# Decay terms of the first attention jobs by matmuls, and earlier loads of the later jobs, in a decay-attention and softplus-FFN kernel

## The chip, the cores and the metric

The kernel runs on one core of one Trainium2 chip. A core has TensorE (PE; matmuls and, beside them, weight loads), VectorE (DVE), ScalarE (ACT), GpSimd (POOL) and SyncE (SP, which here only issues DMA transfers). The metric is the time of one execution on the device, in microseconds; of several executions the median is taken.

## The reference

Attention with a decay over 8 batches of 8 heads, 576 tokens and a head size of 64, and then a feed-forward network with softplus over all 4608 tokens, 512 to 2048 to 512. q, k and f come in float32, the weights in float64. Cut to what is computed:

```
log_f = log(clip(f, 1e-4, 1));  cum = cumsum(log_f, -1)
scores = q @ k^T / 8 + cum[i] - cum[j],  -1e9 above the diagonal
attn = softmax(scores);  x = attn @ v          (heads side by side)
h = x @ w_in;  g = max(h, 0) + log1p(exp(-|h|));  out = g @ w_out
```

## The kernel before

**Numbers.** Most products are split into high and low parts of a faster format (fp32r) and made of two or three matmuls. At the start, while the weights are still arriving, "plain" jobs work in full float32 instead, in which a matmul takes two passes in the trace (a matmul of a transposition one).

**Weights.** w_in and w_out are float64. `load_f64` fetches a piece of 128 x 512 as pairs of words (0.5 MB a piece, 16 of each) into one of five staging buffers and makes float32 of it in five steps: `scale` on ScalarE (L444), `clip` (L447), `low` on GpSimd (L460), `sign` on ScalarE (L464), `join` on VectorE (L468). Later each piece is split into high and low parts (`copy`, L215, into `wih`, and a subtraction, L515).

**Jobs.** Attention is a row of jobs, each with its query tiles. A query tile makes scores (`s`, L787), takes their masked minimum on VectorE (L794; signs are turned, so the minimum is that of the negative scores) and their exponential on ScalarE (L814). Then the weights are turned by matmuls with the identity (`b`, L895, with the reciprocal sums by L899), copied from PSUM (L215) and multiplied by the values (`o`, L968); a product on VectorE (L991) writes x. Batch 0 is cut into three kinds of plain jobs:
- two *first* jobs: 4 heads at once, the first 128 tokens (in the code `quad`)
- four *second* jobs: 2 heads, tokens 128 to 256 (`pair`)
- eight *rests*: one head, tokens 256 to 576, query tiles of 64, 128 and 128 rows; a rest's values came in three steps, one for each bank of turned weights

The other 56 jobs are whole heads in split form. The FFN on the first two blocks of 128 tokens is plain too (up L1158, down L1281), and its up-projections need four converted pieces of w_in at a time. All later blocks are split (L1177, L1262).

**The decay.** f is loaded, clipped (L360), its logarithm taken (L363) and summed along each row by scans on VectorE (first 256 columns L376, the rest L381). `cum["x"]` holds three planes, -8, the sums and 8. Two rows of it are copied by DMA beneath q and k in the tile `T`, as rows 64 and 65, so that a score matmul over 66 rows adds the decay by itself: L691 for the first jobs (two transfers for four heads), L674 for a rest (two transfers).

**The order.** Everything is collected as operations with costs, waits and buffers, and `Plan.run` writes each engine's instructions in the order that its own estimates of their times give; the hardware then runs each engine in that order. Where the planner expects TensorE to wait more than 0.5 us, until the first down-projection, it puts in fill matmuls (`fill`, L1492), which compute nothing. Three `warm` matmuls (L1481) compute nothing either. Transfers are issued by SyncE in order, and an issue that has to wait holds up those behind it. When weight pieces are asked for is set by `W_EACH` at the end of the program.

Of the kernel before, what the change touches and what calls it, by code (L numbers as in the profile page):

```python
# [24 lines left out]
SCALE_BIAS = 1.0  # L25
# [25 lines left out]
class Plan:  # L51
# [109 lines left out]

def on_pe32(n):

    return On("PE", 4 * n / 2400 + 0.004)

# [53 lines left out]
def tile_decay_attention_softplus_ffn(  # L219
# [129 lines left out]

    decay_ready, cum_used, first_rows, cum = {}, [], [], {}  # L350

    def decay():
# [18 lines left out]

        def scan(e):

            c = cum[0]
            x = box["f"][:, 0:256]
            e.tensor_tensor_scan(c[:, 0:256], x, x, 0.0, ALU.add, ALU.min)  # L376

        def scan_rest(e):
            c = cum[0]
            x = box["f"][:, 256:S]  # L380
            e.tensor_tensor_scan(c[:, 256:S], x, x, c[:, 255:256], ALU.add, ALU.min)  # L381

# [39 lines left out]
    def load_f64(src, new, name, takes=()):  # L422
# [29 lines left out]
        def low(e):  # L452
            box["x"] = new()
            out = halves_of(box["x"], 2)[:, :, 0]
            x = halves_of(box["s"].rearrange("p c t -> p (c t)"), 4)[:, :, 1]
            scale, bias = 2.0**-13, 2.0**-14 - 0.5
            if e is nc.scalar:
                e.activation(out, x, AF.Copy, scale=scale, bias=bias)
            else:
                e.tensor_scalar(out, x, scale, bias, ALU.mult, ALU.add)  # L460

# [141 lines left out]
    def attention(job):  # L603
# [65 lines left out]
        def load32():  # L669
            def qk(e):  # L670
                e.dma_start(out=qk32[0:64], in_=qkT[b, :, heads[0]])

            def rows(e, x):
                e.dma_start(out=qk32[64 + x : 65 + x], in_=cum["x"][bh : bh + 1, 1 - x : 3 - x])  # L674

            start = add(NO_ENGINE, mark, takes=("T0",), lag=0.0)
            x = add_dma(qk, 288, after=[start] + first_rows)
            y = [
                add_dma(lambda e, r=r: rows(e, r), 4, after=[start, decay_ready["sums"]] + first_rows)
                for r in range(2)  # L680
            ]
            cum_used.append(add(NO_ENGINE, mark, after=y))
            st["T"] = [x] + y

        def load_quad():
# [81 lines left out]
        def stat_tile(ti):  # L767
# [12 lines left out]
            for i, (a, z, acc) in enumerate(pieces):  # L780
# [3 lines left out]
                def scores(e, box=box, a=a, z=z):  # L784
                    o = box["o"] = bank("att", f"s{n}_{ti}_{a}")[0:n_q, 0 : z - a]
                    if plain:
                        e.matmul(o, part32(0, q0, end), part32(1, a, z), start=True, stop=True)  # L787
                        return
                    e.matmul(o, qA[:, q0:end], kA[:, a:z], start=True, stop=False)  # L789
                    e.matmul(o, qB[0:ST, q0:end], kB[0:ST, a:z], start=False, stop=True)  # L790

                def row_min(e, box=box, w=z - a, i=i, final=final):
# [61 lines left out]
        def weights(bi):  # L854
# [68 lines left out]
            need = list(dict.fromkeys(need)) + halves_set  # L923
            m = add(on_turn(len(blocks) - 0.48 * small + 2 * len(sums)), turn, after=need, takes=("att",))
            st.setdefault("turned", []).append(m)
# [17 lines left out]
        def output_tiled():  # L943

            steps = [[] for _ in banks]
            for gi, (g0, g1, r, c0) in enumerate(groups):
# [10 lines left out]
                for m in mms:  # L957
                    m.update(start=m is mms[0], stop=m is mms[-1])
            box, before = {}, []
            for i, step in enumerate(steps):  # L960
# [3 lines left out]
                def values(e, i=i, step=step):  # L964
# [10 lines left out]
                op = add(  # L975
                    on_pe32(max(sum(m["z"] - m["a"] for m in ms) for ms in sides)), values,
                    after=list(dict.fromkeys(x for m in step for x in m["ready"])) + before + st["V"],
                    takes=("att",) if i == 0 else (),
                )
                before = [op]  # L980
                used[i].append(op)

# [111 lines left out]
    def ffn_block(i):  # L1094
# [48 lines left out]
        def up_part(u, k, half):  # L1143
# [41 lines left out]
            else:  # L1185
                need = st["load"]
            op = add(
                on_pe32(NCC * nt) if plain else on_pe(nt, 6), mm,
                after=st["split"] + need + st["ups"][-1:],
# [292 lines left out]

    give("h", [add(On("PE", 0.75 * WARM), warm, takes=("h",), after=mask_set)])

# [11 lines left out]
    for n in range(len(jobs) + 1):  # L1496
# [89 lines left out]
```

## Time and profile before

| | us |
|---|---|
| median of 3 runs | 1182.69 (1180.13 to 1183.42) |
| the profiled execution's own time | 1187.69 |
| its span, first to last instruction | 1185.9 |
| TensorE busy | 1170.5 (99%) |
| VectorE, ScalarE busy | 799.8 (67%), 832.1 (70%) |
| GpSimd busy | 127.7 (11%) |

The page gives busy time of each engine and the chain of work that ended last. Groups of lines give an operation's busy time, mean duration and the idle time before it. A timeline row has start, length, engine, line, operation, tiles, shape and count; matmuls are counted in passes. Busy time of TensorE includes fills, and a matmul's end is modelled.

### The profile page before, as it was taken

Reading aid. Unit: us, or ns where it says so; the run is one execution under the profiler, and the core shown is the slowest. Engines: PE = TensorE matmul, PEld = TensorE weight load, DVE = VectorE, ACT = ScalarE, POOL = GpSimd, SP = SyncE. Lnnn points to the kernel's source line nnn. Section 1 sums busy time; section 2 is a strip of 40 time slices with the busy share of each in tenths; the row PEclk is TensorE's granted clock in tenths of the full one; section 3 lists DMA queues with packets and bytes.
Section 4 is the critical chain, followed back from the end, with each engine's and each line's share of the span. In section 5 each row is a group of like instructions: output and inputs, shape, how many; then the busy total and the mean of one; then the engine's idle time right before and its main releaser. Section 6 shows DMA issues by size and latency. Waiting matters only on the chain.

```text
span 1185.9 us, 19896 instructions
## 1 busy us (share of the span) xinstructions
PE 1170.5 (99%) x6378; PEld 971.7 (82%) x6378; DVE 799.8 (67%) x1991; ACT 832.1 (70%) x1981; POOL 127.7 (11%) x139
## 2 busy tenths in 40 slices
PE   9999999999999999999999999999999999999998
PEld 7766779878888888888888888888888888888887
DVE  6877898877787678776776678667866773223322
ACT  5877787877886787677867777778767773444543
POOL 4211121110111011110000101001011010000000
PEclk9999999989999999999999999999999999999999
DMA  8856575555566555665566546656566433211210
GB/s 245 243 158 201 163 206 153 143 135 161 156 183 179 174 152 157 181 182 160 147 198 189 149 137 201 179 148 172 149 186 175 137 107 122 89 44 46 89 54 36
DMA packets 120776, 180.39 MB, mean 152 GB/s; under 512 B 22944, under 2 KB 80320, under 8 KB 120672
## 3 DMA queue, kind: packets, MB, share of 16 engines
q1 hardware_dynamic: 120648, 179.11, 52.5%
q8 instruction: 51, 0.84, 0.3%
q14 instruction: 53, 0.43, 0.1%
q10 hardware_dynamic: 24, 0.02, 0.0%
HBM read 109.98 MB, written 35.95 MB: 123 GB/s over the span
## 4 chain that ended last, share of the span: by engine, by line
PE 92%; DVE 4%; ACT 2%; DMA 1%; issue 1%; SPq 0%; POOL 0%; DVEq 0%; ACTq 0%; POOLq 0%
PE h L1177 31%; PE acc L1262 30%; PE b L895 8%; PE o L1027 7%; PE s L789 3%; PE s L790 3%; PE acc L1281 2%; PE h L1158 2%; PE s L787 2%; PE fill L1492 1%; PE o L968 1%; DMA T<-T 1%; ACT p L814 1%; DVE s L794 1%; DVE xl L1129 0%
## 5 line engine op out<-in xcount | busy, mean ns | idle before, releaser
L814 ACT ACTIVATE p<-s,negm 128x288 f32<-128x288 f32 (+7 forms) x384 | 183.3, 480 | 67.7 <-DVE negm L794 65.0
L1177 PE MATMUL h<-xh,wih 128*128 128x512 f32 (+1 forms) x576 | 229.9, 402 | 0.1
L1177 PE MATMUL h<-xl,wih 128*128 128x512 f32 (+1 forms) x576 | 217.7, 381 | 0.0
L794 DVE CUSTOM_DVE_ANT_0 s<-s,cmask 128x288 f32<-128x288 f32 (+6 forms) x320 | 138.0, 440 | 96.7 <-PE s L790 86.8
L1224 DVE SCALAR_TENSOR_TENSOR h<-h,e 128x512 f32<-128x512 f32 x136 | 95.8, 704 | 128.8 <-ACT e L1216 127.7
L844 POOL TENSOR_SCALAR p<-p,rsum 128x448 f32<-128x448 f32 (+4 forms) x85 | 95.1, 1127 | 763.6 <-DVE rsum L828 342.0
L1210 ACT ACTIVATE e<-h 128x512 f32<-128x512 f32 x144 | 86.0, 597 | 120.7 <-PE h L1177 116.5
L1262 PE MATMUL acc<-woh_dt_float32r,gh 128*128 128x512 f32 x376 | 153.1, 407 | 0.0
L1177 PE MATMUL h<-xh,wl 128*128 128x512 f32 (+1 forms) x576 | 149.0, 381 | 0.0
L1262 PE MATMUL acc<-woh_dt_float32r,gl 128*128 128x512 f32 x376 | 147.3, 392 | 0.1
L1262 PE MATMUL acc<-wol_dt_float32r,gh 128*128 128x512 f32 x376 | 146.9, 391 | 0.0
L921 DVE TENSOR_TENSOR pl<-b,ph 128x512 fp32r<-128x512 f32 x168 | 111.0, 666 | 21.0 <-ACT ph L215 17.8
L1177 PEld LDWEIGHTS h<-xh,wl 128*128 128x128 f32 x576 | 105.3, 189 | 21.5
L1177 PEld LDWEIGHTS h<-xh,wih 128*128 128x128 f32 x576 | 109.7, 190 | 15.7 <-PE b L895 0.3
L1177 PEld LDWEIGHTS h<-xl,wih 128*128 128x128 f32 x576 | 109.8, 191 | 14.8 <-DVE xl L1129 0.2
L1232 DVE TENSOR_TENSOR gl<-h,gh 128x512 fp32r<-128x512 f32 x136 | 93.6, 688 | 41.3 <-ACT gh L215 38.9
L895 PE MATMUL b<-ident,p 128*128 128x128 f32 (+1 forms) x728 | 118.5, 270 | 2.7 <-ACT p L215 1.7
L215 ACT CAST ph<-b 128x512 fp32r<-128x512 f32 (+2 forms) x167 | 82.1, 493 | 45.2 <-PE b L895 39.6
L215 ACT CAST gh<-h 128x512 fp32r<-128x512 f32 x113 | 66.4, 588 | 60.5 <-DVE h L1224 41.3
L895 PEld LDWEIGHTS b<-ident,p 128*128 128x128 f32 (+1 forms) x728 | 87.0, 139 | 19.3 <-issue 3.6
L789 PE MATMUL s<-T 128*64 128x64 f32 x336 | 97.6, 304 | 4.7 <-DMA T<-T 2.0
L790 PE MATMUL s<-T 68*64 68x64 f32 x336 | 98.0, 296 | 0.1
(153 smaller groups left out, 2224.0 us busy)
## 6 DMA issues: line engine op xcount, KB each, us to landing
wl<-wil_d SPq DMA_DIRECT2D x72, 512.0 KB
T<-T SPq DMA_DIRECT2D x224, 144.0 KB
raw<-in_qkT SPq DMA_DIRECT2D x112, 144.0 KB
g_d<-gh SPq DMA_DIRECT2D x84, 128.0 KB
g_d<-gl SPq DMA_DIRECT2D x84, 128.0 KB
vr<-in_vR SPq DMA_DIRECT2D x64, 160.0 KB
out<-ob SPq DMA_DIRECT2D x36, 256.0 KB
sto<-in_w_out SPq DMA_DIRECT2D x11, 512.0 KB
```

What stands on the lines that cost most here:

```text
L215: (e.tensor_copy if hasattr(e, "tensor_copy") else e.copy)(out, in_)
L789: e.matmul(o, qA[:, q0:end], kA[:, a:z], start=True, stop=False)
L790: e.matmul(o, qB[0:ST, q0:end], kB[0:ST, a:z], start=False, stop=True)
L794: e.tensor_tensor_reduce(out=box["o"], in0=box["o"], in1=cmask[0:n_q, right - w : right], scale=-0.125, scalar=m0 if i else 3.0e38, op0=AL ...
L814: e.activation(o, box["o"], AF.Exp, bias=m1, scale=-1.0, accum_out=acc)
L844: e.tensor_scalar(a, a, f_, None, ALU.mult)
L895: e.transpose(box["ps"][0 : x.shape[1], at : at + one.shape[1]], x, one)
L921: e.tensor_sub(box["l"], box["ps"][:, 0:w], box["h"].bitcast(F32))
L1177: e.matmul(o, l, r, start=m == 0, stop=m == 11)
L1224: e.scalar_tensor_tensor(h, h, 0.0, box["e"], ALU.max, ALU.add)
L1232: e.tensor_sub(box["l"], box["t"], box["h"].bitcast(F32))
L1262: e.matmul(st["acc", tt], l, r[fc], start=first and m == 0, stop=last and m == 2,)
```

## The change

Five things are changed.

First jobs: the score matmul runs over 64 rows, q and k alone, and two further matmuls into the same bank add the decay: the sums' tile `cum` as the stationary operand against a row of an 8-times identity that is spread over 128 columns, and a spread row of a -8-times identity as the stationary operand against `cum`. Both are float32, 64 rows deep and 128 columns wide; four tiles in two jobs make sixteen of them. They wait for a scan of the first 128 columns alone; the scan is now in three pieces (128, 128, 320). The two rows in `T` are still written for these heads, since the second jobs read them.

Rests: their two rows come in one transfer. Their first query tile multiplies 128 columns of queries instead of 64; the minimum and what follows use the first 64 rows, as before. Their values are one step, after all banks, instead of three.

Loads: before the first rest, one weight piece is asked for per job instead of two.

Planner: no fill before TensorE's first instruction; other costs for `warm`, for `low` (which now also reserves the port that it shares with VectorE), for values, for turned sums and for plain up-projections. `clip` may only go to VectorE, and `low` only to GpSimd.

```
-                elif op.start - clock["PE"] > 0.5:
+                elif clock["PE"] and op.start - clock["PE"] > 0.5:
...
+    eye8 = [cpool.tile([BH, BH], F32, name=f"eye8{x}") for x in "pm"]
+    eye8_set = [
+        add(
+            [on_act(BH), on_dve(BH, True)],
...
+        for x, v in zip(eye8, (8.0, -8.0))
+    ]
...
-        decay_ready["first"] = add(On("DVE", 0.63), scan, after=[l])
-        c = decay_ready["sums"] = add(On("DVE", 0.78), scan_rest, after=[decay_ready["first"]])
+        for x, a, z in (("quad", 0, P), ("first", P, 2 * P), ("sums", 2 * P, S)):
+            on = On("DVE", 0.11 + (z - a) / 480)
+            c = decay_ready[x] = add(on, lambda e, a=a, z=z: scan(e, a, z), after=[c])
...
-        on = [On("POOL", 1.95), on_dve(512, True, bias=SCALE_BIAS)]
-        cl = add(on, clip, after=[sc])
-        lw = add(On("POOL", 1.95), low, after=[ld], takes=takes)
+        cl = add(on_dve(512, True), clip, after=[sc])
+        lw = add(On("POOL", 0.85, 0.0, True), low, after=[ld], takes=takes)
...
             if quad:
-                return heads32(heads[a // P], 1)[0:ST0, 0, which, 0:P]
+                return heads32(heads[a // P], 1)[0:64, 0, which, 0:P]
...
-            def rows(e, x):
-                e.dma_start(out=qk32[64 + x : 65 + x], in_=cum["x"][bh : bh + 1, 1 - x : 3 - x])
+            def rows(e):
+                x = cum["x"][bh : bh + 1, 0:2]
+                planes = bass.AP(x.tensor, x.offset, [x.ap[0], [S, 2], [S, 2], [1, S]])
+                e.dma_start(out=qk32[64:ST0], in_=planes)
...
-            st["T"] = T_of[heads[0]] = T_of[heads[2]] = x + y
+            st["T"] = x
+            T_of[heads[0]] = T_of[heads[2]] = x + y
...
-                        e.matmul(o, part32(0, q0, end), part32(1, a, z), start=True, stop=True)
+                        e.matmul(
+                            o, part32(0, q0, q0 + P), part32(1, a, z), start=True, stop=not quad,
+                        )
...
+                def sums(e, box=box, h=heads[ti % len(heads)]):
+                    c, (plus, minus) = cum[0][:, 0:P], (x[:, h : h + 1].to_broadcast([BH, P]) for x in eye8)
+                    e.matmul(box["o"], c, plus, start=False, stop=False)
+                    e.matmul(box["o"], minus, c, start=False, stop=True)
...
+                if quad:
+                    o = add(on_pe32(2 * P), sums, after=[o, decay_ready["quad"]] + eye8_set)
+                    cum_used.append(o)
...
+            if not quad and not pair:
+                steps = [sum(steps, [])]
...
-            for _ in range(W_EACH if n >= nfirst else W_EACH - 1):
+            for _ in range(W_EACH if n >= nfirst else 1):
```

**Where the order moves.** Names in the rows are tiles with a running number: `s` scores, `T` the q/k tile, `b` turned weights, `o` outputs, `x` attention's result, `sti`, `sto`, `xh_st`, `xl_st` staging buffers, `ti`, `to` pieces on their way, `woh`, `wol` the float32 pieces of w_in and w_out.

TensorE, the start of the program; before:

```order
L1492 MATMUL fill<-cmask 128x128 x4
L1481 MATMUL warm<-cmask 128x448 x3
L1492 MATMUL fill<-cmask 128x128 x13
L787 MATMUL s_0_0_183<-T_72 128x128
L787 MATMUL s_1_128_185<-T_72 128x128
L787 MATMUL s_2_256_187<-T_72 128x128
L787 MATMUL s_3_384_192<-T_72 128x128
L1492 MATMUL fill<-cmask 128x128 x2
L787 MATMUL s_0_0_201<-T_72 128x256
```

The same place in the changed kernel:

```order
L1495 MATMUL warm<-cmask 128x448 x3
L787 MATMUL s_0_0_154<-T_72 128x128
L805 MATMUL s_0_0_154<-eye8p,cum 128x128
L806 MATMUL s_0_0_154<-cum,eye8m 128x128
L787 MATMUL s_1_128_161<-T_72 128x128
L805 MATMUL s_1_128_161<-eye8p,cum 128x128
L806 MATMUL s_1_128_161<-cum,eye8m 128x128
```

The seventeen early fills are gone, and each score of a first job has its two products behind it. In the whole program 3 fill matmuls are left of 58.

SyncE, from the weight pieces six and seven on (the first rest's load is L671, its rows L674, its values L652); before:

```order
L440 DMA sto_321<-in_w_out 128x1024
L440 DMA sto_351<-in_w_out 128x1024
L440 DMA xh_st<-in_w_out 128x1024
L440 DMA xh_st<-in_w_in 128x1024
L440 DMA xl_st<-in_w_in 128x1024
L440 DMA sti_457<-in_w_in 128x1024
L671 DMA T_72<-in_qkT 64x1152
L674 DMA T_72<-cum 1x16x72 x2
L652 DMA vr_499<-in_vR 128x320
```

The same place in the changed kernel:

```order
L444 DMA sto_316<-in_w_out 128x1024
L444 DMA sto_342<-in_w_out 128x1024
L670 DMA T_72<-in_qkT 64x1152
L675 DMA T_72<-cum 2x1x1152
L651 DMA vr_392<-in_vR 128x320
L444 DMA xh_st<-in_w_out 128x1024
L670 DMA T_72<-in_qkT 64x1152
L675 DMA T_72<-cum 2x1x1152
L651 DMA vr_444<-in_vR 128x320
L444 DMA xh_st<-in_w_in 128x1024
L670 DMA T_73<-in_qkT 64x1152
L675 DMA T_73<-cum 2x1x1152
```

The first rest's load now stands behind the seventh weight piece, before behind the eleventh, with one transfer of rows; the last three pieces of the second group of w_in come after the third rest's load.

VectorE, ahead of the first rest's first minimum (the last row of each piece); before:

```order
L468 SCALAR_TENSOR_TENSOR wol_dt_float_435<-to_447,wol_dt_float_435 128x512
L794 ISA s_1_256_466,negm_76<-s_1_256_466,cmask 128x256
L794 ISA negm_76 128x1
L991 TENSOR_TENSOR x_0_261<-o_473,p_1_471 128x128
L447 TENSOR_SCALAR ti_481<-ti_481 128x512
L468 SCALAR_TENSOR_TENSOR woh_dt_float_459<-ti_461,woh_dt_float_459 128x512
L827 SCALAR_TENSOR_TENSOR lsum_80<-lsum_80,part_84 128x2
L828 RECIPROCAL rsum_88<-lsum_80 128x2
L215 CAST wih<-woh_dt_float_459 128x512
L447 TENSOR_SCALAR ti_495<-ti_495 128x512
L468 SCALAR_TENSOR_TENSOR woh_dt_float_483<-ti_481,woh_dt_float_483 128x512
L794 ISA s_0_0_521,negm_77<-s_0_0_521,cmask 64x320
```

In the changed kernel:

```order
L468 SCALAR_TENSOR_TENSOR wol_dt_float_379<-to_386,wol_dt_float_379 128x512
L387 CAST ch<-cum 64x576
L388 TENSOR_TENSOR cl<-cum,ch 64x576
L468 SCALAR_TENSOR_TENSOR wol_dt_float_410<-to_402,wol_dt_float_410 128x512
L1005 TENSOR_TENSOR x_0_256<-o_374,p_1_377 128x128
L797 ISA s_1_256_439,negm_76<-s_1_256_439,cmask 128x256
L797 ISA negm_76 128x1
L797 ISA s_0_0_448,negm_77<-s_0_0_448,cmask 64x320
```

Between the first minimum of all and this row, VectorE had 11 clips, 10 joins, 4 copies into `wih` (L215) and 2 subtractions (L515), and has 7 clips, 7 joins and none of the last two; copies of turned weights are 5 instead of 4. On ScalarE up to the same tile's exponential the scalings are 8 instead of 11, the steps with the sign 7 instead of 11, the copies of turned weights 5 instead of 7, and the copies into `wih` 4 instead of 2.

More of the change, by code (lines that the diff above doesn't have):

```diff
@@ L159, in on_pe, with on_pe32 @@
     return On("PE", times * (max(n * 0.000444, m * 0.00092) + 0.002))
-def on_pe32(n):
-    return On("PE", 4 * n / 2400 + 0.004)
+def on_pe32(n, switch=False):
+    return On("PE", 4 * n / 2400 + 0.004 + 0.19 * switch)
 def on_turn(n):
@@ L350, in tile_decay_attention_softplus_ffn @@
     decay_ready, cum_used, first_rows, cum = {}, [], [], {}
+    eye8 = [cpool.tile([BH, BH], F32, name=f"eye8{x}") for x in "pm"]
+    eye8_set = [
+        add(
+            [on_act(BH), on_dve(BH, True)],
+            lambda e, x=x, v=v: e.mul(x, ident[0:BH, 0:BH], v) if e is nc.scalar
+            else e.tensor_scalar(x, ident[0:BH, 0:BH], v, None, ALU.mult),
+        )
+        for x, v in zip(eye8, (8.0, -8.0))
+    ]
     def decay():
@@ L370, in eights, with scan @@
             e.memset(cum["x"][:, t, :], value)
[L372 to L381, printed above, removed]
+        def scan(e, a, z):
+            c, x = cum[0], box["f"][:, a:z]
+            e.tensor_tensor_scan(c[:, a:z], x, x, c[:, a - 1 : a] if a else 0.0, ALU.add, ALU.min)
         def split(e):
@@ L398, in decay @@
         l = add(on_act(S), log, after=[o])
-        decay_ready["first"] = add(On("DVE", 0.63), scan, after=[l])
         decay_ready["eights"] = set_
-        c = decay_ready["sums"] = add(On("DVE", 0.78), scan_rest, after=[decay_ready["first"]])
+        c = l
+        for x, a, z in (("quad", 0, P), ("first", P, 2 * P), ("sums", 2 * P, S)):
+            on = On("DVE", 0.11 + (z - a) / 480)
+            c = decay_ready[x] = add(on, lambda e, a=a, z=z: scan(e, a, z), after=[c])
         give("wl", [c])
@@ L455, in low @@
             x = halves_of(box["s"].rearrange("p c t -> p (c t)"), 4)[:, :, 1]
[L456 to L460, printed above, removed]
+            e.tensor_scalar(out, x, 2.0**-13, 2.0**-14 - 0.5, ALU.mult, ALU.add)
         def sign(e):
@@ L671, in qk @@
                 e.dma_start(out=qk32[0:64], in_=qkT[b, :, heads[0]])
-            def rows(e, x):
-                e.dma_start(out=qk32[64 + x : 65 + x], in_=cum["x"][bh : bh + 1, 1 - x : 3 - x])
+            def rows(e):
+                x = cum["x"][bh : bh + 1, 0:2]
+                planes = bass.AP(x.tensor, x.offset, [x.ap[0], [S, 2], [S, 2], [1, S]])
+                e.dma_start(out=qk32[64:ST0], in_=planes)
             start = add(NO_ENGINE, mark, takes=("T0",), lag=0.0)
             x = add_dma(qk, 288, after=[start] + first_rows)
[L678 to L683, printed above, removed]
+            y = add_dma(rows, 9, after=[start, decay_ready["sums"]] + first_rows)
+            cum_used.append(add(NO_ENGINE, mark, after=[y]))
+            st["T"] = [x, y]
         def load_quad():
@@ L784, in scores @@
                 def scores(e, box=box, a=a, z=z):
-                    o = box["o"] = bank("att", f"s{n}_{ti}_{a}")[0:n_q, 0 : z - a]
+                    o = bank("att", f"s{n}_{ti}_{a}")[:, 0 : z - a]
+                    box["o"] = o[0:n_q]
                     if plain:
-                        e.matmul(o, part32(0, q0, end), part32(1, a, z), start=True, stop=True)
+                        e.matmul(
+                            o, part32(0, q0, q0 + P), part32(1, a, z), start=True, stop=not quad,
+                        )
                         return
+                    o = box["o"]
                     e.matmul(o, qA[:, q0:end], kA[:, a:z], start=True, stop=False)
@@ L923, in weights @@
             need = list(dict.fromkeys(need)) + halves_set
-            m = add(on_turn(len(blocks) - 0.48 * small + 2 * len(sums)), turn, after=need, takes=("att",))
+            m = add(on_turn(len(blocks) - 0.48 * small + 2 * len(sums) + 1.7 * bool(sums)), turn, after=need, takes=("att",))
             st.setdefault("turned", []).append(m)
@@ L975, in output_tiled @@
                 op = add(
-                    on_pe32(max(sum(m["z"] - m["a"] for m in ms) for ms in sides)), values,
+                    on_pe32(max(sum(m["z"] - m["a"] for m in ms) for ms in sides), True), values,
                     after=list(dict.fromkeys(x for m in step for x in m["ready"])) + before + st["V"],
@@ L980, in output_tiled @@
                 before = [op]
-                used[i].append(op)
+                for bi in range(len(banks)) if len(steps) == 1 else (i,):
+                    used[bi].append(op)
             puts = []
@@ L1187, in up_part @@
             op = add(
-                on_pe32(NCC * nt) if plain else on_pe(nt, 6), mm,
+                on_pe32(1.05 * NCC * nt) if plain else on_pe(nt, 6), mm,
                 after=st["split"] + need + st["ups"][-1:],
@@ L1481, in warm @@
             e.matmul(o[:, 0:MW], cmask[:, 0:P], cmask, start=True, stop=True)
-    give("h", [add(On("PE", 0.75 * WARM), warm, takes=("h",), after=mask_set)])
+    give("h", [add(On("PE", 1.3 * WARM), warm, takes=("h",), after=mask_set)])
     filling = []
```

## The prediction

> **What bounds the kernel now.** I read the page first: span, busy shares, the chain that ended last.
>
> ```profile
> span 1185.9 us, 19896 instructions
> PE 1170.5 (99%) x6378; PEld 971.7 (82%) x6378; DVE 799.8 (67%) x1991; ACT 832.1 (70%) x1981; POOL 127.7 (11%) x139
> PE 92%; DVE 4%; ACT 2%; DMA 1%; issue 1%; SPq 0%; POOL 0%; DVEq 0%; ACTq 0%; POOLq 0%
> ```
>
> TensorE is the bound: 99% busy, 92% of the chain. The matmuls that compute something are the same before and after, apart from sixteen new ones and the width of eight. So the time can only change where TensorE is idle, runs matmuls that compute nothing, or runs slowly. I looked for these with the windows (in each row: length, then busy time of PE, weight loads, DVE, ACT and POOL, granted clock, DMA share, GB/s) and with the groups of lines.
>
> ```profile
> 0.00:80.00 80.00, 75.79 (x535) 55.73 (x536) 62.03 (x188) 58.48 (x141) 23.40 (x41) 1.00 0.72 212
> 80.00:140.00 60.00, 60.00 (x409) 41.74 (x409) 48.09 (x119) 45.45 (x101) 11.99 (x15) 1.00 0.66 192
> L1492 PE MATMUL fill<-cmask 128*128 128x128 f32 x116 | 16.5, 292 | 1.4 <-POOL cmask L314 1.4
> L1481 PE MATMUL warm<-cmask 128*128 128x448 f32 x6 | 4.2, 863 | 0.0
> ```
>
> In the first 80 us TensorE is idle for 4.2 us, fills for 16.5 and warms for 4.2: 24.9 us without result. From 80 to 140 it is never idle. What the change can win by an earlier start lies in these 24.9 us. The timeline shows where the first of them are.
>
> ```profile
> 1.39 2.07 PE L1492 MATMUL fill<-cmask 128*128 128x128 f32 x8 [1.39 <-POOL cmask L314]
> 3.26 4.19 PE L1481 MATMUL warm<-cmask 128*128 128x448 f32 x6
> 7.28 3.06 PE L1492 MATMUL fill<-cmask 128*128 128x128 f32 x26
> 10.18 1.06 PE L787 MATMUL s<-T 66*128 66x128 f32 x8
> 36.29 3.39 PE L1492 MATMUL fill<-cmask 128*128 128x128 f32 x28
> 39.62 0.75 PE L787 MATMUL s<-T 66*64 66x320 f32 x2
> 116.03 0.75 PE L787 MATMUL s<-T 66*64 66x320 f32 x2
> ```
>
> The first score starts at 10.18, the first rest's first score at 39.62, both right behind a run of fills. I take the stretches between these marks; the second ends at 116.03, where the eighth rest starts.
>
> ```profile
> 10.18:39.62 29.44, 28.07 (x225) 21.99 (x223) 26.26 (x83) 24.02 (x62) 11.07 (x12) 1.00 0.87 276
> 39.62:116.03 76.41, 74.96 (x513) 51.40 (x512) 58.37 (x149) 60.63 (x132) 17.36 (x22) 1.00 0.66 193
> ```
>
> In the first stretch VectorE is busy 89% and ScalarE 82%: with the weights' conversions between the first jobs' steps, these two set its length. In the second TensorE does.
>
> **The start.** The first scores no longer wait for the two rows that are written after the scan, only for q and k. The next rows show when these can be there (the last three are of the transfers: two sizes, and the issue of weight pieces six and seven).
>
> ```profile
> 2.00:5.50 3.50, 3.50 (x10) 2.27 (x10) 1.40 (x3) 0.69 (x2) 1.61 (x8) 1.00 0.85 206
> 1.73 0.30 POOL L335 TENSOR_SCALAR_AFFINE_SELECT cmask<-cmask 128x128 f32<-128x128 f32 x1
> 4.66 0.68 DVE L376 TENSOR_TENSOR_SCAN cum<-fs 64x256 f32<-64x256 f32 x1 [0.75 <-ACT fs L363]
> 10.73 0.30 DVE L794 CUSTOM_DVE_ANT_0 s<-s,cmask 128x128 f32<-128x128 f32 x1 [4.17 <-PE s L787]
> fs<-in_f SPq DMA_DIRECT2D x1, 144.0 KB
> T<-in_qkT SPq DMA_DIRECT2D x4, 256.0 KB
> 15.92 2.07 SPq L440 DMA_DIRECT2D sto<-in_w_out  x2
> ```
>
> By 5.5 us 3.5 x 206 = 0.72 MB have moved; f (0.15 MB) and the first two q/k transfers (0.26 each), issued first, are 0.67. The scan of 256 columns ended at 5.34, that of 128 ends sooner, so the products' new wait is over before the scores, behind which they stand. With the early fills gone, the warm matmuls start when cmask is ready, at 2.1, and take their 4.2 us to 6.3. So the first score starts at about **6.6 instead of 10.18**. The sixteen products have two passes each; 26 passes of this size took 3.06 us, 0.118 each, so 32 x 0.118 = 3.8 us of TensorE. They lie in the stretch that VectorE and ScalarE set, where fills took their place before. A tile takes 0.7 us now; the first minimum is at 7.4 instead of 10.73, VectorE having waited 4.17 us there. The eye tiles and the split scan run on engines that wait there; if that cover were gone, they would cost about 0.5 us.
>
> **The stretch to the first rest.** The rows of the order on VectorE say which conversions move behind it: from the first minimum to the first rest's, 7 clips instead of 11, 7 joins instead of 10, no copies of w_in's high part instead of 4, no subtractions instead of 2, one copy of turned weights more. On ScalarE 3 scalings, 4 steps with the sign and 2 copies of turned weights fewer, 2 copies of high parts more. Rows for their durations (least, median, largest, in ns):
>
> ```profile
> L447 DVE TENSOR_SCALAR ti<-ti x16: 409/422/993, 16.3 to 99.3; 128x512 f32<-128x512 f32 x16
> L468 DVE SCALAR_TENSOR_TENSOR woh_dt_float<-ti,woh_dt_float x16: 670/686/1176, 18.9 to 101.6; 128x512 uint32<-128x512 uint32 x16
> L215 DVE CAST wih<-woh_dt_float x9: 410/427/1035, 23.2 to 102.3; 128x512 fp32r<-128x512 f32 x9
> L515 DVE TENSOR_TENSOR wil<-woh_dt_float,wih x10: 662/683/693, 25.9 to 137.4; 128x512 fp32r<-128x512 f32 x10
> L215 DVE COPY p<-b x13: 409/553/684, 15.1 to 130.9; 128x384 f32<-128x384 f32 x9, 128x512 f32<-128x512 f32 x3, 128x256 f32<-128x256 f32 x1
> L444 ACT ACTIVATE ti<-sti x9: 667/675/682, 15.2 to 98.4; 128x512 f32<-128x512 f32 x9
> L464 ACT ACTIVATE woh_dt_float<-ti x16: 759/777/790, 17.5 to 100.7; 128x512 f16<-128x512 f32 x16
> L215 ACT COPY p<-b x23: 342/561/588, 14.3 to 132.1; 128x512 f32<-128x512 f32 x13, 128x384 f32<-128x384 f32 x7, 128x256 f32<-128x256 f32 x3
> L215 ACT CAST wih<-woh_dt_float x7: 592/619/621, 28.4 to 97.2; 128x512 fp32r<-128x512 f32 x7
> ```
>
> VectorE: 4 x 0.42 + 3 x 0.69 + 4 x 0.43 + 2 x 0.68 - 0.55 = 6.3 us less, 26.26 - 6.3 = 20.0; at the same 89%, 22.4 us. ScalarE: 3 x 0.675 + 4 x 0.777 + 2 x 0.56 - 2 x 0.62 = 5.0 less, 19.0; at 82%, 23.2 us. The larger: the first rest starts at 6.6 + 23.2 = 29.8, **9.8 us earlier**. Ends of this term: 10.6 if VectorE alone sets it; 3.6 if only the start moves and the rest keeps its 29.4 us. I take ScalarE's, the nearer to what these engines reached before. The rest's data isn't late: its load is issued behind the seventh weight piece instead of the eleventh, and pieces six and seven were issued by 18 us.
>
> **From there to the eighth rest** TensorE has the same work. Before, it lost 76.41 - 74.96 = 1.45 us idle and the fills of this row:
>
> ```profile
> 40.00:60.00 20.00, 1.87 (x12) 1.49 (x12) 1.00 0.77 230
> ```
>
> Together 3.3 us, of which I take half as gained: **1.6** (ends 0 and 3.3). Against it stand the deferred conversions: ScalarE has 60.63 + 5.0 = 65.6 us to do in about 74, 89%, a share like those at which the first stretch was held up. I charge **1.6** (ends 0 and 3). That rows go in one transfer saves an issue on SyncE per rest, whose data isn't late: nothing. A rest's values in one step wait for its last copied bank; TensorE has next scores and up-projections ahead of them in the order, and without these one copy, 0.55 us, would show per rest: nothing.
>
> The first tile of a rest now uses 128 columns of queries instead of 64. Two tiles show what the narrow one costs:
>
> ```profile
> 105.67 0.75 PE L787 MATMUL s<-T 66*64 66x320 f32 x2
> 106.36 1.98 PE L1281 MATMUL acc<-wol_dt_float,g 128*128 128x512 f32 x4
> 109.16 0.92 PE L787 MATMUL s<-T 66*128 66x448 f32 x2
> 109.92 1.02 PE L1281 MATMUL acc<-wol_dt_float,g 128*128 128x512 f32 x2
> ```
>
> Start to start, the wide tile has 0.76 us for two passes of 448, so 320 would take 0.54; the narrow one has 0.69. By eight rests the extra 0.15 and about 0.1 behind it are **2.0 us** gained (ends 0 and 2.9).
>
> **The clock.** The fills also kept TensorE busy. Where it wasn't, this happened:
>
> ```profile
> 175.00:180.00 5.00, 3.35 (x19) 3.10 (x18) 3.12 (x10) 3.32 (x10) 2.64 (x2) 0.75 0.70 202
> PE s L789 <- DMA T<-T: 2.0, 2, 1.6
> 160.00:260.00 100.00, 94.59 (x579) 83.20 (x577) 84.80 (x229) 78.55 (x207) 15.63 (x14) 0.95 0.56 152
> ```
>
> One wait of 1.6 us, and the granted clock was 0.75 over these five: TensorE stood 1.65 us and then had half its speed for a while. Between 7 and 30 us the work is 29.44, less 1.4 idle and the 9.5 us of fills there (16.5 - 2.1 - 3.1 - 1.9 elsewhere), 18.5, and 3.8 of products: 22.3 of 23.2, but in pieces. I charge **1.6 us** for a spell at half clock that isn't hidden (ends 0 and 10). The Trainium skill (TensorE: Matmul & The Clock Gate, section HAM oscillation) asks only that no gap of TensorE exceeds about 3.4 us; by it the fills can go for nothing, and the sum would be 1.6 us better. The trace differs: a wait of 1.6 was enough.
>
> **Sum:** 9.8 + 1.6 + 2.0 - 1.6 - 1.6 = 10.2 us. The profiled execution took 1187.7 us, so the changed one should take 1177.5. The median of the runs shown, 1182.69, is 5.0 lower; taken from it, the forecast is **1172.5 us**, 0.9% faster.
>
> **Rivals.**
> *The weights become the bound.* Rests load ahead of weights, and SyncE waits in order: behind a rest's load that waits for its buffer stand the pieces for the second group of up-projections. For it: the DMA share is 0.87 already in the first stretch, and that group's last pieces stand behind the third rest's load. Against it: their results are needed only after the second rest. If most of the start's gain is waited away, some 3.6 us + 2.0 stay, less the two charges: 2.4, so 1180.3.
>
> *The change doesn't do what it says:* the products take what the rows' wait gave (3.8 against 3.6) and VectorE and ScalarE hold the rest where it was. Then only the first tiles' 2.0 is left: 1180.7, within 0.3% (3.5 us), which is about what a measurement of this kernel tells from no change.
>
> *Slower: half clock through the first jobs.* Fills gone, the scattered work falls under what keeps the clock up, and stays there. Then its 22.3 us take 44.6, the first rest starts at 51.2 instead of 39.6, and less 2.0 + 1.6 the total is 8.0 us worse: 1190.7. It decides once the first rest starts later than 43.2, that is with 14.3 of the 22.3 us of work at half speed. For it: the 175 to 180 row. Against it: in that row PE was busy 67%, and from 0 to 80, without the fills, still (75.79 - 16.5) / 80 = 74%; and a slow TensorE is busier, which brings the clock back.
>
> *Another planned order later.* From 160 to 260 TensorE is idle 5.4 us and 5% of the clock is missing, 10.4 us in all. All later rows are planned anew from other times; this loss may be 5 us larger or smaller.
>
> **How the numbers follow.** Forecast, within the spread of the last rival (1167.5 to 1177.5): 0.56. More gained (10.6 at the rest, 3.3, 2.9, no charges: 16.8, so 1166): 0.10. Weights: 0.16. Only the tiles: 0.10. Half clock, or the later loss at its worst with little gained: 0.08. To hold 8 in 10, the range runs from **1165** to **1182**. Faster by over 0.3% (below 1179.1): the forecast, the better case and about half of the weights (that case loses less than all of it as often as not), 0.74; within: 0.18; slower: 0.08.
>
> **What would show it.** First score at 6 to 7 us, the first minimum 3 us earlier, the first rest's score between 28 and 33, fill time near zero, the eighth rest between 103 and 110, granted clock 1.00 in the first 40 us. The clock below that from 10 to 30 would show the slower rival; long waits of the up-projections (L1158 before) for a weight piece would show the first. If the eighth rest is 9 us earlier and the end isn't, the loss after 160 us has grown.

## The result and the profile after

| | before | after |
|---|---|---|
| median of 4 runs each | 1182.39 (1180.13 to 1183.42) | 1168.51 (1167.36 to 1168.53) |
| the profiled execution's own time | 1187.69 | 1167.36 |
| its mean granted clock | 0.995 | 0.999 |

The ratio is 0.9878, 95% interval 0.9859 to 0.9896: 13.9 us faster by the medians, where 10.2 were forecast. The page of the changed kernel, with span, busy times and the chain that ended last:

```profile
span 1165.6 us, 19711 instructions
PE 1154.2 (99%) x6300; PEld 960.4 (82%) x6300; DVE 796.9 (68%) x1992; ACT 832.6 (71%) x1984; POOL 126.8 (11%) x138
PE 85%; DVE 4%; ACT 1%; issue 0%; DVEq 0%; ACTq 0%
```

TensorE's busy time fell by 16.3 us: 110 fill passes are gone and the products' 32 are new, which is the whole difference from x6378 to x6300. Now the same stretches as before the change; the windows of the changed kernel (length, then busy time of PE, weight loads, DVE, ACT, POOL, then granted clock, DMA share, GB/s):

```profile
0.00:80.00 80.00, 76.72 (x531) 54.90 (x531) 64.05 (x194) 64.84 (x153) 23.24 (x41) 1.00 0.79 236
80.00:140.00 60.00, 58.60 (x409) 42.90 (x408) 54.38 (x142) 50.63 (x121) 12.68 (x17) 1.00 0.72 202
6.41:31.06 24.65, 23.78 (x184) 17.78 (x184) 19.25 (x72) 19.97 (x56) 7.04 (x8) 1.00 0.82 242
31.06:103.54 72.48, 72.15 (x510) 51.55 (x508) 61.18 (x159) 62.87 (x140) 20.26 (x25) 1.00 0.79 236
160.00:260.00 100.00, 98.36 (x604) 86.71 (x603) 88.62 (x238) 83.39 (x215) 14.93 (x13) 0.98 0.57 158
```

And its timeline on TensorE at the marks of the prediction (start, length, engine, line, operation):

```profile
2.08 4.40 PE L1495 MATMUL warm<-cmask 128*128 128x448 f32 x6 [2.08 <-POOL cmask L335]
6.41 0.48 PE L787 MATMUL s<-T 64*128 64x128 f32 x2
6.73 0.38 PE L805 MATMUL s<-eye8p,cum 64*128 64x128 f32 x2
6.96 0.38 PE L806 MATMUL s<-cum,eye8m 64*128 64x128 f32 x2
9.28 0.94 PE L1506 MATMUL fill<-cmask 128*128 128x128 f32 x6
30.52 1.24 PE L787 MATMUL s<-T 66*128 66x256 f32 x4
103.54 0.70 PE L787 MATMUL s<-T 66*128 66x320 f32 x2
```

The first score starts at 6.41 instead of 10.18. The first rest's first score is the second half of the row at 30.52 and starts at 31.06 instead of 39.62; the eighth rest starts at 103.54 instead of 116.03. So the gain builds up in three pieces: 3.8 us by the first score, 4.8 more to the first rest (24.65 for 29.44), 3.9 more to the eighth (72.48 for 76.41): 12.5. Of the profiled executions' other 7.8 us (spans 1185.9 and 1165.6), most lies between 160 and 260, where TensorE is idle for 1.6 us instead of 5.4 and has 0.98 of its clock instead of 0.95. But the profiled execution of before was 5.3 us above its median, so of these 7.8 only some 1.4 belong to the medians' 13.9 (13.9 - 12.5).

### The profile page after: what moved, and what is told of

The parts are those of the page before. It is cut to its first block, busy times and chain, and to the rows that moved or that the text cites. A ratio compares the mean times of both kernels' runs of the same rounds, so it can differ in the third digit from the quotient of the medians.

```text
span 1165.6 us, 19711 instructions
## 1 busy us (share of the span) xinstructions
PE 1154.2 (99%) x6300; PEld 960.4 (82%) x6300; DVE 796.9 (68%) x1992; ACT 832.6 (71%) x1984; POOL 126.8 (11%) x138
## 4 chain that ended last, share of the span: by engine, by line
PE 85%; DVE 4%; ACT 1%; issue 0%; DVEq 0%; ACTq 0%
PE h L1191 32%; PE acc L1276 31%; PE b L906 7%; PE o L1041 7%; PE s L793 3%; PE s L792 3%; PE acc L1295 1%; DVE s L797 1%; DVE xl L1143 1%; DVE pl L932 0%; DVE h L1238 0%; DVE x L1067 0%; DVE wil L514 0%; PE h L1172 0%; ACT p L825 0%
## 5 line engine op out<-in xcount | busy, mean ns | idle before, releaser
L215 ACT CAST ph<-b 128x512 fp32r<-128x512 f32 (+2 forms) x169 | 82.8, 491 | 44.3 <-PE b L906 34.6
L215 ACT CAST gh<-h 128x512 fp32r<-128x512 f32 x111 | 65.2, 587 | 58.4 <-DVE h L1238 39.1
```

The costliest lines, as they stand in the source:

```text
L215: (e.tensor_copy if hasattr(e, "tensor_copy") else e.copy)(out, in_)
```

## The experiments

Twelve kernels ran, in 4 to 12 executions each. Three questions: does the clock hang on what keeps TensorE busy at the start (theory C of the expectations); how much of the gain do the early start and the loads carry; and do the planner's side (costs, one step for a rest's values) and the first tile's width matter? Times are medians; the last columns are of the profiled execution. In e9 and e10 the first score is the first matmul that computes one, behind the matmuls without a result (dummies) that run ahead of it, and the first rest is read from the same place of the order. The ratio isn't the quotient of the medians: long executions move it (c1's medians, 1167.49 and 1182.01 for before beside it, would give 0.988).

| run | us | ratio to before, 95% | first score | first rest |
|---|---|---|---|---|
| c1, the change again | 1167.49 | 0.9905 (0.9875 to 0.9936) | 5.99 | 30.94 |
| e1, narrow first tile | 1168.29 | 0.9884 (0.9871 to 0.9896) | 6.85 | 31.92 |
| g1, more fills | 1168.81 | 0.9881 (0.9863 to 0.9898) | 6.74 | 32.85 |
| e2, without the products | 1176.06 | 0.9941 (0.9923 to 0.9960) | 6.52 | 37.52 |
| e9, dummies for the products | 1170.63 | 0.9907 (0.9887 to 0.9927) | 7.71 | 34.1 |
| e5, rows again | 1178.13 | 0.9947 (0.9924 to 0.9969) | 11.60 | 42.67 |
| e10, rows and dummies | 1173.19 | 0.9922 (0.9906 to 0.9938) | 11.47 | 35.72 |
| e4, two weight pieces per job | 1177.50 | 0.9969 (0.9947 to 0.9991) | 6.62 | 36.02 |
| e7, values in three steps | 1176.50 | 0.9946 (0.9927 to 0.9965) | 6.67 | 31.25 |
| e8, old planner costs | 1176.38 | 0.9947 (0.9933 to 0.9961) | 8.06 | 36.73 |
| e3, before without fills | 1189.16 | 1.0065 (1.0052 to 1.0078) | 9.37 | 41.61 |
| e6, before with the loads alone | 1178.65 | 0.9957 (0.9939 to 0.9974) | 10.21 | 34.38 |

### c1 and e1: the change again, and its first tile narrow

> The changed kernel as it is, beside the next three on the same chip. Both theories: about 1168.5 us, 13.9 less than before.

1166.1 to 1168.5 in six executions; three others took 1173.6, 1176.1 and 1183.1, the first two at a mean clock of 0.994 and 0.991, so the new kernel too loses its clock at times. The third had 0.999; what made it long is not known.

```
-                            o, part32(0, q0, q0 + P), part32(1, a, z), start=True, stop=not quad,
+                            box["o"], part32(0, q0, end), part32(1, a, z), start=True, stop=not quad,
```

> The changed kernel, with the first query tile of a rest 64 columns wide again; the order of all instructions stays. If the narrow tile costs 0.25 us each time (0.15 itself, 0.1 behind it), the time is 2.0 us above the changed kernel's. The rival, that those 0.25 us came from other neighbours in the trace and not from the width: within 0.5 us of the changed kernel.

1168.29 for 1168.51: no difference. From the first to the eighth rest it takes 73.3 us instead of 72.5, so the wide tile saves 0.8 us there and not the 2.0 of the prediction, and even that doesn't reach the end.

### e2 and e9: the products, as cover for the clock

e2 leaves out the sixteen products (the first jobs lack their decay) at the same order:

```
-                            o, part32(0, q0, q0 + P), part32(1, a, z), start=True, stop=not quad,
+                            o, part32(0, q0, q0 + P), part32(1, a, z), start=True, stop=True,
...
-                    e.matmul(box["o"], c, plus, start=False, stop=False)
-                    e.matmul(box["o"], minus, c, start=False, stop=True)
```

> The changed kernel without its sixteen products, so that the first jobs lack their decay; the order of all else stays. If the products lie where VectorE and ScalarE set the pace, as the prediction said, the time changes by less than 1 us. If they lie on the path, up to their 3.6 us (16 x 0.223 in the changed kernel's timeline) go.

Less work, and 8 us slower, which neither side expected. The windows of e2 show why, and below them its longest waits on TensorE between 6.7 and 33.4 us (total, times, longest):

```profile
9.60:13.01 3.41, 2.53 (x19) 1.49 (x17) 1.72 (x9) 1.64 (x7) 0.00 (x0) 0.99 0.97 241
13.01:33.49 20.48, 20.11 (x85) 12.48 (x85) 16.15 (x48) 15.05 (x36) 6.56 (x8) 0.50 0.64 213
33.49:40.00 6.51, 6.51 (x50) 4.75 (x49) 3.81 (x12) 3.88 (x10) 0.00 (x0) 1.00 0.44 131
```

```profile
PE s L787 <- DMA T<-in_qkT: 0.9, 1, 0.9
PE s L787 <- ACT p L823: 0.7, 1, 0.7
PE b L904 <- ACT p L823: 0.4, 1, 0.4
```

From 9.60 to 13.01 TensorE was busy 74%, with no wait over 0.9 us; then it ran at half clock for 20.48 us, although it was busy 98% of them. Of its six executions, one had a mean clock of 0.999 and took 1169.6, the other five 0.989 to 0.993 and 1175.5 to 1178.0: with the clock up, by this one execution, the products' absence costs 1 us at most, and the other 7 are the clock.

e9 puts two matmuls without a result ahead of each first job's score in e2:

```
+                        for _ in range(2 * quad):
+                            e.matmul(o, cmask[:, 0:P], cmask[:, 0:P], start=True, stop=True)
                         e.matmul(
                             o, part32(0, q0, q0 + P), part32(1, a, z), start=True, stop=True,
```

> The changed kernel without its sixteen products (so the first jobs lack their decay terms), with two dummy matmuls of the mask's 128 columns ahead of each of the first eight scores: TensorE gets the same amount of work at these places, none of it with a result. Theory C (the products' worth beside the start is that they keep TensorE busy enough for full clock): the clock stays 1.00 in the first 40 us, the first rest starts at 30 to 32 us, 1166.5 to 1169.5 us. Theory P (the loss of 8 us without the products came from something else than a less busy TensorE, such as another course of VectorE's minima): the clock falls to half again and it takes 1174 to 1178.

The same stretch in e9:

```profile
0.00:20.00 20.00, 17.93 (x86) 12.09 (x86) 8.57 (x43) 8.51 (x26) 6.12 (x22) 1.00 0.86 226
20.00:40.00 20.00, 19.46 (x138) 12.41 (x138) 19.17 (x62) 19.05 (x48) 4.21 (x5) 1.00 0.70 198
```

Its first score stands behind four passes of stand-ins:

```profile
6.72 1.06 PE L788 MATMUL s<-cmask 128*128 128x128 f32 x4
7.71 0.71 PE L789 MATMUL s<-T 64*128 64x128 f32 x2
```

The clock is 1.00 again and 5.4 us of the 8 come back. Of the six executions four held the clock (0.999 to 1.000, 1169.5 to 1170.7); the other two had 0.994 and 0.995 and took 1175.8 and 1173.7. The first rest comes at 34.1, later than the 30 to 32 expected: VectorE gets through 8.57 us of work in the first 20, for 11.6 in the changed kernel, so the stand-ins ahead of the scores aren't as well placed as the products behind them. So a busy TensorE is what the products give to the clock, whatever they compute; that is theory C, with a price of its own for the stand-ins and 1.1 us above the time that it expected.

### e3 and g1: the fills

e3 is the kernel before with its 58 fills left out, nothing else.

```
...
-        for _ in range(round(us / 0.215)):
-            e.matmul(filling[0][:, 0:P], cmask[:, 0:P], cmask[:, 0:P], start=True, stop=True)
+        pass
```

> The kernel before without its 58 fills, all else in the same order. Theory A, the fills overran their gaps and pushed real work back: 3 to 6 us faster than before. Theory B, the work behind them waited for data or for VectorE and ScalarE anyway: within 1 us of before. Theory C, they kept the clock up: the granted clock falls to 0.5 in windows between 10 and 40 us and the time is up to 5 us longer.

Windows of e3, and the longest wait on TensorE from 6 to 40 us:

```profile
0.00:20.00 20.00, 15.09 (x49) 9.37 (x50) 8.84 (x46) 8.88 (x28) 6.98 (x23) 0.74 0.82 242
20.00:40.00 20.00, 18.38 (x96) 13.10 (x95) 15.06 (x40) 12.84 (x30) 5.05 (x7) 0.58 0.66 185
40.00:60.00 20.00, 17.87 (x100) 12.07 (x98) 15.19 (x43) 14.52 (x33) 6.04 (x7) 0.83 0.82 246
```

```profile
PE s L787 <- DMA T<-cum: 2.8, 1, 2.8
```

Half clock for 27.3 us from 9.6 and for 6.8 from 47.2, and 7 us slower, 2 more than theory C allowed. The wait that the early fills of before covered shows bare: the first scores stood 2.8 us for the rows of the sums. So in the kernel before the fills held the clock in the first 40 us. That the clock makes up all of the 7 us isn't shown: four of the five executions had a mean clock of 0.984 to 0.986 and took 1187.7 to 1190.7, but the fifth had 0.996 and took 1190.9, the longest.

g1 has fills in the changed kernel again, wherever the planner expects 0.05 us of wait (12 instead of 3).

```
-                elif clock["PE"] and op.start - clock["PE"] > 0.5:
+                elif clock["PE"] and op.start - clock["PE"] > 0.05:
...
-        for _ in range(round(us / 0.215)):
+        for _ in range(max(1, round(us / 0.215))):
```

> The changed kernel with nine single fills more, between 16 and 45 us; the order of all else stays. If the changed kernel's few longer executions (1173 to 1183 among 1166 to 1168.5) come from the clock falling in the first 40 us, they get rarer here; the usual executions stay at 1166 to 1169, since the fills stand where TensorE waits. If the fills are on the path, all executions are up to 2 us longer (9 x 0.22).

1168.81: no gain. Its four executions lie between 1168.1 and 1170.8 at clocks of 0.999 and 1.000; four are too few to say that it never loses the clock.

### e5 and e10: the start without the products

e5 takes the decay of the first jobs from rows of `T` again, so the first scores wait for them.

```
-                return heads32(heads[a // P], 1)[0:64, 0, which, 0:P]
+                return heads32(heads[a // P], 1)[0:ST0, 0, which, 0:P]
...
-            st["T"] = x
-            T_of[heads[0]] = T_of[heads[2]] = x + y
+            st["T"] = T_of[heads[0]] = T_of[heads[2]] = x + y
...
-                if quad:
-                    o = add(on_pe32(2 * P), sums, after=[o, decay_ready["quad"]] + eye8_set)
-                    cum_used.append(o)
```

> The changed kernel, but the first jobs read their decay from the two rows beneath q and k again, without the products; loads, planner costs and all else of the change stay, and the planner puts in 15 fills. By the prediction's start term the first score falls back to about 10 us and the first rest by up to 3.6 us: 1169 to 1172. The rival, that the products' gain is only that they keep TensorE busy: fills do the same here, and the time is within 1 us of 1168.5.

10 us slower, which neither side expected, and again two kinds of executions: two of ten at a mean clock of 1.000 took 1169.4 and 1170.1, the other eight at 0.988 to 0.991 took 1175.8 to 1181.0. In the profiled one the clock is half for 23.9 us:

```profile
14.30:38.20 23.90, 23.90 (x101) 14.72 (x101) 16.30 (x53) 16.21 (x43) 6.07 (x7) 0.50 0.52 165
```

e10 adds the dummies of e9 to e5:

> The changed kernel with the first jobs' decay terms as rows of the q/k tile again, and the same two dummy matmuls ahead of each of the first eight scores. Theory C: the start is as late as with the rows alone (11 to 12 us), the clock now holds, the first rest starts at 33 to 36, and it takes 1169 to 1172: the earlier start itself is worth 1 to 4 us, and the other 8 of the 10 that the rows cost were the clock. Theory S (the earlier start is itself worth 8 us or more, and the clock is a side matter): 1175 to 1180 even with the clock at 1.00.

The timeline of e10 (fills, dummies, first score):

```profile
6.71 3.31 PE L1504 MATMUL fill<-cmask 128*128 128x128 f32 x22
9.86 0.61 PE L787 MATMUL s<-cmask 128*128 128x128 f32 x4
11.47 0.46 PE L788 MATMUL s<-T 66*128 66x128 f32 x2 [1.00 <-DMA T<-cum]
```

The clock held, and it took 1173.2, 1.2 above the range expected and 2.6 us more than e9, for a first score 3.8 us later (11.47 for 7.71). e5's two executions at full clock say 1 to 2 us. So **the earlier start itself is worth 1 to 3 us**, with the order that the planner makes of it; the other 7 to 9 that the rows cost in e5 are the clock. Theory S falls. In the profiled executions the later start is made up by the eighth rest, which starts at 107.51 in e10 and 107.72 in e9, so that the difference arises behind it; how much the start alone is worth stays open within these bounds.

### e4 and e6: the loads

e4 asks for two weight pieces per job ahead of the first rest again; e6 is before with one.

```
-            for _ in range(W_EACH if n >= nfirst else 1):
+            for _ in range(W_EACH if n >= nfirst else W_EACH - 1):
```

> The changed kernel, but two weight pieces asked for per job ahead of the first rest, as before; the planner orders anew and puts in 22 fills instead of 3. If the deferred conversions are what brought the first rest forward (the first stretch is set by VectorE and ScalarE), the first rest starts 3 to 5 us later than 31.1 and the time is about 1171 to 1174. If the start alone did it, the first rest stays within 1 us and the time at 1168.5.

> The kernel before with one part of the change alone: one weight piece per job ahead of the first rest instead of two; 36 fills instead of 58. If the deferred conversions are worth what the first stretch's sum says without the start (9.8 less 3.6), the first rest starts about 6 us earlier and the time is 1175 to 1178. If they are given back later, as they have to be done at some time, within 1.5 us of before.

e4 gives back 9 us by the medians, more than the 2.5 to 5.5 expected, and e6 wins 4 to 5. Not all of e4's 9 are the loads: five of its twelve executions, at a clock of 0.998 to 1.000, took 1174.7 to 1175.9, which is 6 to 7 us above the change; six took 1177.4 to 1183.9 at 0.991 to 0.997, and one 1189.3 at 0.999. From first score to first rest, e4 takes 29.4 us (36.02 - 6.62), e6 24.2 (34.38 - 10.21), where before took 29.4 and after 24.65: the loads alone make this stretch, independent of the products. How they do it shows on TensorE in e4:

```profile
26.36 3.84 PE L1172 MATMUL h<-x,woh_dt_float 128*128 128x128 f32 x32
33.46 2.72 PE L1506 MATMUL fill<-cmask 128*128 128x128 f32 x22
36.02 0.70 PE L787 MATMUL s<-T 66*128 66x320 f32 x2
```

and on the queue of transfers, where the first rest's q and k are issued, in e4:

```profile
27.34 0.55 SPq L670 DMA_DIRECT2D T<-in_qkT x1
```

and in the changed kernel, beside its up-projection:

```profile
17.68 0.55 SPq L670 DMA_DIRECT2D T<-in_qkT x1
```

```profile
25.43 3.84 PE L1172 MATMUL h<-x,woh_dt_float 128*128 128x128 f32 x32
```

The up-projection in front of the rest starts only 0.9 us later in e4 (26.36 for 25.43). Then the changed kernel goes on with the first rest's scores, while e4 has 26 fill passes ahead of them: q and k are issued 9.7 us later, behind four more weight pieces, and the planner expects TensorE to wait here. The trace has this transfer as 64 packets of 4608 bytes. The last of them ends at 23.55 us in the changed kernel, at 33.50 in e4 and at 33.95 in the kernel before. So in e4 the last 22 fill passes began just as q and k were there, and the scores came 2.5 us later, behind them; in the kernel before, the 28 passes began at 36.29, 2.3 us after it. Most of this term is then a wait that the planner writes into TensorE's order, and only about 1 us work that ScalarE and VectorE no longer do first. What these scores would have waited for without the fills, if for anything, no run shows.

### e7 and e8: one step for the values, and the planner's costs

```
-            if not quad and not pair:
-                steps = [sum(steps, [])]
```

> The changed kernel with a rest's values in three steps again, one per bank, in place of one; the rest planned anew from there. My theory (one step neither gains nor costs, as predicted): 1166 to 1170. Rival (switching less often between values and other work saves 0.2 to 0.4 us for each of the rests): 1171 to 1176.

8 us slower, the rival's side and just above its range. Up to the first rest nothing changes (31.25); the loss is spread behind it. Windows of e7:

```profile
20.00:60.00 40.00, 38.18 (x280) 27.29 (x280) 35.37 (x95) 34.64 (x81) 12.40 (x15) 1.00 0.75 236
60.00:140.00 80.00, 76.51 (x535) 56.34 (x536) 71.59 (x181) 63.42 (x148) 17.79 (x19) 1.00 0.71 207
140.00:260.00 120.00, 115.10 (x696) 97.24 (x695) 102.89 (x279) 97.51 (x256) 18.83 (x17) 0.99 0.58 156
```

and of the changed kernel:

```profile
20.00:60.00 40.00, 39.35 (x289) 28.21 (x288) 36.09 (x101) 35.67 (x84) 13.19 (x14) 1.00 0.73 230
60.00:140.00 80.00, 78.60 (x547) 57.57 (x546) 70.71 (x182) 68.19 (x157) 16.59 (x22) 1.00 0.74 210
140.00:260.00 120.00, 118.36 (x730) 103.19 (x729) 105.35 (x285) 100.83 (x261) 17.90 (x15) 0.99 0.60 164
```

TensorE is idle for 10.2 us in e7 and 3.7 in the changed kernel, 6.5 more of the 9.7 by which the two profiled executions differ. The waits are for many things, at most 2.1 us for any one (exponentials, values' copies, a high part). Little of the loss lies in the rests themselves. The first job behind them starts in e7 at

```profile
116.81 0.59 PE L792 MATMUL s<-T 128*64 128x64 f32 x1
```

and in the changed kernel, 2.7 us earlier, at

```profile
114.08 0.59 PE L792 MATMUL s<-T 128*64 128x64 f32 x1
```

The other 6.9 of the 9.6 us between the spans (1175.2 and 1165.6) come behind this place. The rival's reason, less switching in each rest, would put the loss in the rests; this speaks for the other order of TensorE that the planner writes for all that follows. A run with one step and the old order was not made, so the two were not separated.

e8 has the planner's old numbers:

```
-    return On("PE", 4 * n / 2400 + 0.004 + 0.19 * switch)
+    return On("PE", 4 * n / 2400 + 0.004)
...
-        lw = add(On("POOL", 0.85, 0.0, True), low, after=[ld], takes=takes)
+        lw = add(On("POOL", 1.95), low, after=[ld], takes=takes)
...
-    give("h", [add(On("PE", 1.3 * WARM), warm, takes=("h",), after=mask_set)])
+    give("h", [add(On("PE", 0.75 * WARM), warm, takes=("h",), after=mask_set)])
```

and likewise the old fill rule, turn and up-projection.

> The changed kernel with the planner's old costs and rules (fill rule, switch, low half of a weight, turn of the sums, up-projections); the work is the same, the order is planned from the old numbers, with 30 fills of 128 columns instead of 3. Theory L (the gain comes from the products and the loads; the costs matter by 3 us at most): 1167 to 1171. Rival (the new costs set a better order, by which much of the gain after 160 us comes): 1173 to 1180.

The rival's time again, 8 us, but not at its place: it looked behind 160 us, and most of the loss is at the start. Windows and timeline of e8:

```profile
8.06:36.73 28.67, 27.01 (x215) 21.98 (x215) 22.16 (x70) 19.87 (x54) 8.41 (x8) 1.00 0.71 198
```

```profile
1.40 2.08 PE L1506 MATMUL fill<-cmask 128*128 128x128 f32 x8 [1.40 <-POOL cmask L314]
3.26 3.98 PE L1495 MATMUL warm<-cmask 128*128 128x448 f32 x6
7.08 1.05 PE L1506 MATMUL fill<-cmask 128*128 128x128 f32 x8
8.06 0.48 PE L787 MATMUL s<-T 64*128 64x128 f32 x2
```

Fills ahead of the warm matmuls and behind them make the first score 1.65 us later, though its data doesn't call for it, and the stretch to the first rest is 4.0 longer. Which of the costs does the latter was not tried.

**Taken together** the parts don't add up: undone one at a time, the loads, the one step and the costs each give back 8 to 9 us (the loads 6 to 7 where the clock holds), and the products 8 to 10, mostly through the clock, of a gain of 13.9. Each part needs the others to be worth what it is; no version that ran is measurably faster than the change.

## Why the prediction was right, and where it wasn't

**The start** held: 6.41 for 6.6, and the scan and the first minimum stand where they were put. VectorE in the changed kernel:

```profile
4.67 0.42 DVE L383 TENSOR_TENSOR_SCAN cum<-fs 64x128 f32<-64x128 f32 x1 [0.75 <-ACT fs L372]
7.50 0.30 DVE L797 CUSTOM_DVE_ANT_0 s<-s,cmask 128x128 f32<-128x128 f32 x1 [0.69 <-PE s L806]
```

The sums were there at 5.1, before the scores, and the minimum came at 7.50 for 7.4. That the sixteen products are hidden held too (e2 at full clock). What the term left out: of 3.8 us gained at the start, 1 to 3 reach the end (e10, e5).

**The stretch to the first rest** was forecast at 23.2 us and took 24.65: 8.6 us gained at the first rest for 9.8. ScalarE had 19.97 us of work at 81%, close to the 19.0 at 82% of the sum. But the reason was only partly right. The sum divides ScalarE's work by its busy share, as if its conversions alone held the first rest; e4, with the old loads, shows 0.9 us of later work and 3.4 us of fills. The step "the rest's data isn't late" was true of the changed kernel and, by the packets, of the kernel before when its 28 fill passes began: these passes were the planner's. The number came out because the same edit removes both, which is luck as far as this reason goes.

**From there to the eighth rest** 3.9 us were gained for a net 2.0. The terms: fills and idle time gave 3.0 (fills gone, idle 0.33 for 1.45), not half of 3.3; the deferred conversions cost nothing visible (ScalarE busy 87%, TensorE idle 0.33 us), not 1.6; the narrow tile was 0.8 by e1's stretch, not 2.0, about 0.1 for each of eight rests where 0.25 was charged, and nothing of it reaches the end.

**The clock** was the right worry. The changed kernel ran at 1.00 through the first 140 us, so the 1.6 us charged weren't paid there; c1's two executions at 0.991 and 0.994 show that a spell can still come. What averts it in most executions is the products themselves: without them (e2, e5) the clock was half for 20 to 24 us in most executions, and 7 us or more were lost. The slower rival's mechanism exists, but smaller than priced: it had all of the first jobs' work at half speed and the first rest at 51.2, and it needed one later than 43.2 to be slower than before. The spells of e2 and e5 covered most of that stretch, and the first rest came at 37.5 and 42.7. Its counter-argument, that a slow TensorE is busier and so the clock comes back, failed: e2 was busy 98% of a spell of 20.48 us.

**"A rest's values in one step: nothing"** is the step that failed: e7 puts it at 8 us. The argument looked at one rest alone, at what its values wait for, and not at what the planner does with TensorE's order afterwards. **The planner's new costs** weren't priced at all; e8 puts them at 8 as well. Both sit in the rival "another planned order later", which was given 5 us either way and no side.

**The weights** never became the bound: TensorE's waits for a plain up-projection (L1172) are 0.3 us in all from 20 to 260, put down to VectorE and not to a weight piece. So the forecast of 1172.5 missed by 4.0 us, on the side of too little, from the two charges that weren't paid, the fills' other half and the later stretches; its parts were less independent than a sum of terms makes them look. That it came this close is partly luck: two parts that give back 8 us each when undone stood in the sum at nothing or not at all.

## What to carry to other kernels

Matmuls without a result that fill TensorE's waits are not waste until the same place is shown to stay busy without them: remove the wait and the fills together, or put real work there, and look at the granted clock. When loads are put into another order, look in the old order at when the data landed and whether fills still stand ahead of its reader then: fills follow the planner's estimate, and not the transfer. Where a planner writes the order, changed costs and merged steps are edits of their own, with effects as large as those of the work they describe, and worth a run each before the parts are added up.

## What the runs showed of the hardware

The granted clock fell to half for multiples of 3.41 us: 20.48 in e2 (six times 3.41), 27.3 and 6.8 in e3 (eight and two), 23.9 in e5 (seven). In the 3.41 us before e2's spell TensorE was busy 74%, with one wait of 0.9 us; in e4 3.41 us that were busy 58% (64.41 to 67.82, with a wait of 1.4) had full clock behind them. So neither a least busy share nor a longest wait can be read from these rows. At half clock, e2 was busy 98% of the spell's 20.48 us, by the trace's modelled ends of matmuls, and the clock still took that long to return. The Trainium skill (TensorE: Matmul & The Clock Gate, section HAM oscillation) puts such drops down to a wait that crosses a window of about 3.4 us; e2's trace differs, with no wait over 0.9. And the same kernel falls or doesn't: one of e2's six executions and two of e5's ten kept their clock.
